# Pooled attention and two MLPs on one core: the order of weight conversion, u3 and the first evacuation in the second MLP

## The chip, the cores and the metric

One core of one Trainium2 chip runs the whole program. The metric is device time in microseconds (us) of one execution; lower is better. Engines are called as in the profile: PE is TensorE (matmul), DVE is VectorE, ACT is ScalarE, POOL is GpSimd, SP is the queue that issues the loads.

## What is computed

```python
q_pool = q.reshape(B, H, S // 2, 2, D).mean(axis=3)
attn = softmax(scale * q_pool @ k^T);  x = (attn @ v)          # 1152 tokens x 512
h = x @ w_in;  r = np.maximum(h, 0.0);  g = s * (r * r) + b    # 512 -> 2048
x = g @ w_out                                                  # 2048 -> 512
a = x @ w_a;  b = x @ w_b;  out = (a * b) @ w_out2             # 512 -> 1536 -> 512
```

[...]

## The kernel before

Every product is made from two parts of each operand: a rounded part h and the rest l, as h*h + h*l + l*h, three matmuls into one PSUM sum (`mm3`, L616). A **unit** is one megabyte of float64 weights. `units` (L104) lists 34 of them: 16 of the first MLP (index 0 to 15), 12 of the second (16 to 27, alternating w_a and w_b), 6 of the last matrix. Converting unit i has two phases, which the generator `conv_phases` (L177) hands out one after the other:

- **bits** (L187): ACT scales the upper words into the tile f (L143), DVE shifts (L145) and joins the lower words (L147), SP's next load is issued (`unit_load`, L128), and for the second MLP DVE makes four sums of blocks (`conv_sums`, L149).
- **split** (L196): ACT rounds f into wh and the sums into sh (L168), DVE or POOL makes wl and sl (L173).

The first MLP walks over `order1`, one unit per step i, two column blocks (mm 0 and 1) per step; in the last steps DVE adds the PSUM results into xacc (L741). `mlp1` yields "split" at the start of a step and "bits" behind the first column block, and the loop at L853 answers each with one conversion phase (two at step 14). So split and bits of coming units stand in the engines' queues between the evacuations: program order is each engine's order here (`manual_schedule`). Behind the evacuations x2's parts are made for the second MLP (`x_sums`, L782): casts x2h on ACT (L772), differences on DVE (L776, L769).

The second MLP multiplies 2 by 2 blocks by seven products instead of eight (p1 to p7, table `FORM`, L833), 12 matmuls of 288 columns each, accumulated in four PSUM pairs of banks. Its unit n (0 to 11) is index 16 + n of the list, odd n are w_b. From n = 1 on the loop at L969 writes PE's order p1, p6, p2, p7, p5, p4, p3. Between the products stand the evacuations: u1 copied by ACT (L848), u2 and **u3** added by DVE (`add_up`, L851), and four results `to(n, i, z)`. p4 accumulates on the bank pair that u3 is read from, so p4 waits for u3. For odd n each result is multiplied by the one of the unit before, by POOL (`times`, L922); the first result, `evac11` (L916), is an exception: for odd n DVE multiplies it straight from PSUM, for even n ACT copies it.

During unit n the conversion of unit n + 1 runs: DVE's L145 and L147 at its start, the sums behind u2, ACT's wh and sh behind these, DVE's wl in two halves of 512 columns, sl (x2l for odd units) on POOL. p6 of unit n + 1 reads sl. The tile f of these units lies in PSUM.

Of the kernel before, what the change touches and what calls it, by code (L numbers as in the profile page):

```python
# [9 lines left out]
F32 = mybir.dt.float32  # L10
F32R = mybir.dt.float32r
I32 = mybir.dt.int32
I64 = mybir.dt.int64
AF = mybir.ActivationFunctionType
ALU = mybir.AluOpType
# [27 lines left out]
def kernel(  # L43
# [14 lines left out]
    nc = tc.nc  # L58
# [4 lines left out]
    SP = S // 2  # L63
# [7 lines left out]
    HC = SP // 2  # L71
# [9 lines left out]
    sp_ps = [ctx.enter_context(tc.tile_pool(name="sp0", bufs=1))]  # L81
    cv_ps = [ctx.enter_context(tc.tile_pool(name="cv0", bufs=1))]
# [21 lines left out]
    units = []  # L104
# [6 lines left out]
    for up, c, u in order1:  # L111
        if up:
            w = w_in[:, c * 512 + u * 256:c * 512 + (u + 1) * 256]
        else:
            w = w_out[c * 512:(c + 1) * 512, u * 256:(u + 1) * 256]
        units.append([(slice(0, 1024), w.rearrange("(k p) f -> p k f", p=128))])
    N1 = len(units)
# [6 lines left out]
    raw_t = {}  # L124
# [3 lines left out]
    def unit_load():  # L128
        i = st["load"]
        z = (i + 1) % 2 if i else 0  # L130
        if i >= len(units) or z >= len(raw_ps):
            return
        t = raw_ps[z].tile([128, 1024], I64, tag="raw", name="raw")
        for c, src in units[i]:
            nc.sync.dma_start(out=t[:, c].rearrange("p (k f) -> p k f", f=src.shape[-1]), in_=src)
        raw_t[i] = t
        st["load"] += 1

    def conv_bits(f, raw):
        words = raw.bitcast(I32).rearrange("p (n t) -> p n t", t=2)  # L140
        lo, hi = words[:, :, 0], words[:, :, 1]

        nc.scalar.activation(out=f.bitcast(F32), in_=hi.bitcast(F32), func=AF.Prelu, scale=2.0 ** -112, alpha=2.0 ** 32)  # L143
        yield
        nc.vector.tensor_scalar(out=f, in0=f, scalar1=3, scalar2=None, op0=ALU.logical_shift_left)  # L145
        yield
        nc.vector.scalar_tensor_tensor(out=f, in0=lo, scalar=29, in1=f, op0=ALU.logical_shift_right, op1=ALU.bitwise_or)  # L147

    def conv_sums(f, t):  # L149

        f = f.bitcast(F32).rearrange("p (k f) -> p k f", k=4)
        a11, a12, a21, a22 = (f[:, 2 * y:2 * y + 2, 128 * x:128 * x + 128] for x in range(2) for y in range(2))
        if f.space == PSUM:
            a = ss_ps[0].tile([128, 2, 128], F32, tag="a21", name="a21")
            nc.scalar.copy(out=a, in_=a21)
        else:
            a = a21
        yield
        for out, x, y, op in (
            (t[:, 1], a11, a, ALU.subtract), (a21, a22, a, ALU.add),  # L160
            (t[:, 0], a22, t[:, 1], ALU.subtract), (t[:, 2], a12, t[:, 0], ALU.subtract),
        ):
            nc.vector.tensor_tensor(out=out, in0=x, in1=y, op=op)  # L163
            yield

    def round_h(h, f, eng):
        if eng is nc.scalar:
            nc.scalar.copy(out=h, in_=f)  # L168
        else:
            nc.gpsimd.tensor_scalar(out=h, in0=f, scalar1=1.0, scalar2=0.0, op0=ALU.mult, op1=ALU.add)  # L170

    def round_l(l, f, h, eng):
        eng.tensor_tensor(out=l, in0=f, in1=h.bitcast(F32), op=ALU.subtract)  # L173

    w2_at = {}

    def conv_phases():  # L177

        for i in range(len(units)):
            in_psum = N1 + 2 <= i <= N2  # L180
            if in_psum:
                f = ps2[3].tile([128, 2, 512], F32, tag="pp", name="f").rearrange("p a n -> p (a n)").bitcast(I32)
            else:
                f = cv_ps[i % len(cv_ps)].tile([128, 1024], I32, tag="f", name="f")
            t = ss_ps[i % 2].tile([128, 3, 2, 128], F32, tag="t", name="t") if N1 <= i < N2 else None

            def bits():  # L187
                yield from conv_bits(f, raw_t.pop(i))
                unit_load()
                yield  # L190
                if i < N1:
                    yield
                if t is not None:
                    yield from conv_sums(f, t)

            def split_up():  # L196
                eng = nc.gpsimd if i < N1 - 1 else nc.scalar
                if i < N2 + 2:
                    p = sp_ps[i % 2]
                    parts = tuple(p.tile([128, 1024], F32R, tag=f"w{x}", name=f"w{x}") for x in "hl")  # L200
                else:
                    parts = w2_room[i - N2 - 2]
                x = f.bitcast(F32)
                round_h(parts[0], x, eng)
                yield
                more = ()
                if t is not None:
                    if i % 2:
                        more = tuple(x[:, 0:768].rearrange("p (z k f) -> p z k f", z=3, k=2) for x in x_room["odd"])
                    else:  # L210
                        more = tuple(ss_ps[0].tile([128, 3, 2, 128], F32R, tag=f"s{x}", name=f"s{x}") for x in "hl")
                    round_h(more[0], t, eng)
                    yield
                if i < N2:
                    sp_t.append(parts + more)
                else:
                    for k in range(2):
                        w2_at[2 * (i - N2) + k] = [x[:, 512 * k:512 * k + 512] for x in parts]
                if in_psum:
                    for c in (slice(0, 512), slice(512, 1024)):  # L220
                        round_l(parts[1][:, c], x[:, c], parts[0][:, c], nc.vector)
                        yield
                else:
                    round_l(parts[1], x, parts[0], nc.vector if t is not None else nc.gpsimd)
                    yield
                if t is not None:
                    round_l(more[1], t, more[0], nc.gpsimd if in_psum else nc.vector)
                    yield

            yield bits()  # L230
            yield split_up()

    ss_ps, w2_room, x_room, ps2 = [], [], {}, []
    phases = conv_phases()
# [2 lines left out]
    def conv_step(n=1, steps=conv):  # L237
        for _ in range(n):
            next(steps, None)
# [386 lines left out]
    with tc.manual_schedule():  # L626
# [193 lines left out]
        def halves(t):  # L820
            return t.rearrange("p (a n) -> p a n", a=2)
# [14 lines left out]
        def product(ps, w, name, first=True):  # L836
            a, x = FORM[name]
            for k in range(2):
                mm3([ps[:, i, 0:HC] for i in range(2)], [t[:, k] for t in w[a]], x_at(x, k), first and k == 0, k == 1, first is not True)
# [72 lines left out]
        def to(n, i, z):  # L912
            p, mul = divmod(n, 2)
            return halves((ab_at(2 * p + i) if mul else at[i])[:, z * SP:(z + 1) * SP])

        def evac11(n, ps):  # L916
            if n % 2:
                nc.vector.tensor_tensor(out=to(n, 0, 0), in0=ps[:, :, 0:HC], in1=halves(at[0][:, 0:SP]), op=ALU.mult)
            else:
                nc.scalar.copy(out=to(n, 0, 0), in_=ps[:, :, 0:HC])  # L920

        def times(n, i, z):  # L922
            if n % 2:
                nc.gpsimd.tensor_tensor(
                    out=to(n, i, z), in0=to(n, i, z), in1=halves(at[i][:, z * SP:(z + 1) * SP]), op=ALU.mult
                )
# [42 lines left out]
        for n in range(1, NU):  # L969

            w = unit_blocks()
            last = n == NU - 1
            a = pair(2)
            product(a, w, "p1")
            if n > 1:
                conv_step(2, ahead)
            copy_up("u1", a)
            b = pair(1)
            product(b, w, "p6")
            if n > 1:  # L980
                conv_step(1, ahead)
            add_up(u_tile("u2"), b, U["u1"])
            conv_step(9, ahead)
            ahead = next(phases)
            conv_step(3 if last else 2, ahead)
            product(a, w, "p2", False)
            if last:
                ab_split(0)
            else:
                conv_step(1, ahead)  # L990
            product(b, w, "p7", False)
            add_up(u_tile("u3"), b, U["u1"])
            conv_step(9, ahead)
            c = pair(0)
            product(c, w, "p5")
            add_up(to(n, 1, 1), c, U["u3"])
            times(n, 1, 1)
            evac11(n, a)
            if last:
                ab_split(1)  # L1000
            product(b, w, "p4", False)
            add_up(to(n, 1, 0), b, U["u1"])
            times(n, 1, 0)
            product(c, w, "p3", False)
            ahead = next(phases)
            conv_step(1, ahead)
            add_up(to(n, 0, 1), c, U["u2"])
            times(n, 0, 1)
# [63 lines left out]
```

## Time and profile before

| what | value |
|---|---|
| median of 3 runs | 711.39 us (709.99 to 711.54) |
| profiled execution, its own time | 711.81 us |
| span of that execution | 710.0 us |
| PE busy | 681.6 us, 96% of the span |
| DVE, ACT, POOL busy | 528.6 us (74%), 396.2 us (56%), 371.9 us (52%) |
| mean granted clock of PE | 0.992 |

The profile is one execution; its rows give start and length in us from the start of the span. A bracket behind a row tells how long the engine was idle before it and which instruction ended that. Consecutive equal instructions are merged in a row, with their count.

### The profile page before, as it was taken

The numbers are of one execution on the slowest core, as the hardware profiler recorded it, in microseconds if no ns is written. First come the engines' busy times: TensorE is split into PE (matmuls) and PEld (weight loads), VectorE is DVE, ScalarE is ACT, GpSimd is POOL, SyncE is SP. The second block draws the span as 40 slices with busy tenths as digits, with TensorE's granted clock in tenths as the row PEclk, the third lists the DMA queues.
The fourth block names the chain that finished last, engine by engine and source line by source line (L and its number), as shares of the span: only waits on it lengthen the run. The fifth ranks groups of instructions, "written<-read, shape, count | busy, mean of one in ns | idle before, by whom it ended". The sixth has DMA issues, their size and how long they took to land.

```text
span 710.0 us, 11849 instructions
## 1 busy us (share of the span) xinstructions
PE 681.6 (96%) x4446; PEld 651.0 (92%) x4446; DVE 528.6 (74%) x963; ACT 396.2 (56%) x861; POOL 371.9 (52%) x372
## 2 busy tenths in 40 slices
PE   7999999999999999999999999988899999999994
PEld 6899999999999989999999999978899999988883
DVE  5999999999999995774375465589778787887430
ACT  5998999999999984553343224135243333444220
POOL 4879797988879775683545455100332433142200
PEclk9999999999999999999999999999999999999998
DMA  6122120302121004322323131310232222322012
GB/s 225 35 67 66 38 69 31 102 12 91 35 67 35 1 24 140 107 88 72 106 63 117 60 119 59 119 60 0 74 105 81 98 91 89 98 96 104 0 47 86
DMA packets 26013, 52.93 MB, mean 75 GB/s; under 512 B 1636, under 2 KB 2916, under 8 KB 25956
## 3 DMA queue, kind: packets, MB, share of 16 engines
q1 hardware_dynamic: 25826, 52.04, 22.4%
q8 instruction: 35, 0.57, 0.3%
q14 instruction: 22, 0.18, 0.1%
q10 hardware_dynamic: 130, 0.13, 0.1%
HBM read 49.81 MB, written 2.36 MB: 73 GB/s over the span
## 4 chain that ended last, share of the span: by engine, by line
PE 71%; DVE 18%; ACT 6%; issue 2%; POOL 1%; DMA 0%; DVEq 0%; ACTq 0%
PE ps L623 26%; PE pp L907 10%; PE pp L623 9%; PE pv L508 9%; PE t L474 7%; PE s L399 6%; PE s L406 3%; DVE p3l L492 2%; DVE t L163 2%; DVE u L851 2%; ACT wh L168 2%; DVE sm L425 2%; PE t L344 1%; DVE wl L173 1%; DVE f L145 1%
## 5 line engine op out<-in xcount | busy, mean ns | idle before, releaser
L474 PE MATMUL t<-ident,e 128*128 128x128 f32 x648 | 98.6, 275 | 3.1 <-DVE p2l L492 1.3
L457 POOL TENSOR_SCALAR e<-e,sm 128x1152 f32<-128x1152 f32 x72 | 88.7, 1233 | 11.5 <-DVE sm L452 6.7
L474 PEld LDWEIGHTS t<-ident,e 128*128 128x128 f32 x648 | 75.2, 140 | 13.5 <-DVE sm L430 2.2
L732 POOL TENSOR_SCALAR r<-r,sb_s,sb_b 128x384 f32<-128x384 f32 (+1 forms) x46 | 41.1, 906 | 55.2 <-DVE r L729 55.2
L422 DVE TENSOR_REDUCE sm<-s 128x1 f32<-128x768 f32 x72 | 68.2, 948 | 1.8 <-PE s L399 1.8
L492 DVE TENSOR_TENSOR p3l<-t,p3h 128x512 fp32r<-128x512 f32 (+1 forms) x120 | 64.2, 553 | 7.0 <-ACT p3h L486 4.5
L441 ACT ACTIVATE e<-s,sm 128x768 f32<-128x768 f32 x72 | 66.5, 924 | 0.0
L486 ACT CAST p3h<-t 128x512 fp32r<-128x512 f32 (+1 forms) x120 | 56.2, 485 | 5.5 <-PE t L474 3.2
L173 POOL TENSOR_TENSOR sl<-t,sh 128x768 fp32r<-128x768 f32 x5 | 9.2, 1843 | 90.8 <-ACT sh L168 90.8
L726 ACT ACTIVATE r<-ps 128x384 f32<-128x384 f32 (+1 forms) x46 | 20.1, 505 | 61.7 <-PE ps L623 61.6
L623 PE MATMUL pp<-x2h,wh 128*128 128x288 f32 x192 | 43.5, 308 | 10.5 <-DVE u L851 5.4
L729 DVE SCALAR_TENSOR_TENSOR r<-ps,r 128x384 f32<-128x384 f32 (+1 forms) x46 | 23.8, 567 | 37.1 <-ACT r L726 37.1
L492 DVE TENSOR_TENSOR p2l<-t,p2h 128x512 fp32r<-128x512 f32 x96 | 50.6, 548 | 1.0 <-ACT p2h L486 0.8
L173 POOL TENSOR_TENSOR wl<-f,wh 128x1024 fp32r<-128x1024 f32 x17 | 42.9, 2525 | 9.4 <-ACT wh L168 8.2
L486 ACT CAST p2h<-t 128x512 fp32r<-128x512 f32 x96 | 44.8, 501 | 5.1 <-PE t L474 4.5
L508 PE MATMUL pv<-p3h,v 128*128 128x320 f32 x144 | 47.6, 338 | 0.0
L434 ACT ACTIVATE e<-s,sm 128x384 f32<-128x384 f32 x72 | 43.0, 597 | 7.5 <-DVE sm L452 3.5
L143 ACT ACTIVATE f<-raw 128x1024 f32<-128x1024 f32 x34 | 38.7, 1139 | 14.4 <-issue 6.7
L145 DVE TENSOR_SCALAR f<-f 128x1024 int32<-128x1024 int32 x34 | 37.9, 1116 | 11.6 <-ACT f L143 11.5
L147 DVE SCALAR_TENSOR_TENSOR f<-raw,f 128x1024 int32<-128x1024 int32 x34 | 45.6, 1342 | 1.1
L623 PE MATMUL ps<-xa_h,wh 128*128 128x384 f32 (+1 forms) x200 | 45.3, 330 | 0.1
L623 PE MATMUL ps<-xa_h,wl 128*128 128x384 f32 (+1 forms) x200 | 45.0, 328 | 0.0
(144 smaller groups left out, 2095.5 us busy)
## 6 DMA issues: line engine op xcount, KB each, us to landing
raw<-in_moe_w_out_dram SPq DMA_DIRECT2D x14, 1024.0 KB, 4.9
raw<-in_moe_w_in_dram SPq DMA_DIRECT2D x8, 1024.0 KB, 5.6
raw<-in_moe_w_a_dram SPq DMA_DIRECT2D x6, 1024.0 KB, 5.0
raw<-in_moe_w_b_dram SPq DMA_DIRECT2D x6, 1024.0 KB, 5.6
vn<-in_v_dram SPq DMA_DIRECT2D x8, 576.0 KB, 3.9
kn<-in_k_dram SPq DMA_DIRECT2D x7, 576.0 KB, 3.9
qn<-in_q_dram SPq DMA_DIRECT2D x7, 512.0 KB, 3.7
out_dram<-ab SPq DMA_DIRECT2D x8, 256.0 KB, 2.7
```

The lines of the kernel that those rows point to most:

```text
L145: nc.vector.tensor_scalar(out=f, in0=f, scalar1=3, scalar2=None, op0=ALU.logical_shift_left)
L147: nc.vector.scalar_tensor_tensor(out=f, in0=lo, scalar=29, in1=f, op0=ALU.logical_shift_right, op1=ALU.bitwise_or)
L173: eng.tensor_tensor(out=l, in0=f, in1=h.bitcast(F32), op=ALU.subtract)
L422: nc.vector.reduce_max(small(g)[:, 0:1], SPS[g, 0][:, :, 0:384], axis=AX.XY)
L441: nc.scalar.activation(out=e_tile(g)[:, 0:768].rearrange("p (a c) -> p a c", a=2), in_=SPS.pop((g, 0))[:, :, 0:384], func=AF.Exp, bias=m[: ...
L457: nc.gpsimd.tensor_scalar(out=e, in0=e, scalar1=m[:, 6:7], scalar2=1.0, op0=ALU.mult, op1=ALU.mult)
L474: nc.tensor.transpose(ps[:, i * 128:(i + 1) * 128], E[g][:, (c0 + i) * 128:(c0 + i + 1) * 128], ident)
L486: nc.scalar.copy(out=p_dst(g)[0][:, c0:c0 + n], in_=p_src(g, z))
L492: nc.vector.tensor_tensor(out=l, in0=p_src(g, z), in1=h.bitcast(F32), op=ALU.subtract)
L508: nc.tensor.matmul(ps[:, 0:N], V[n, hd][:, c].rearrange("p a d -> p (a d)"), p, start=(t == 0), stop=(t == 2 * NC - 1))
L623: nc.tensor.matmul(ps, a, c[:, o:o + n], start=(first and z == 0), stop=(last and z == 2), skip_group_check=more)
L907: nc.tensor.matmul(ps, a[x], w2_at[kf][c], start=(kf == 0 and y == 0), stop=(kf == KF2 - 1 and y == 2))
```

## The change

Three things. First, the order in which `conv_phases` hands out the phases: for index 16 the split is kept back until the bits of index 17 are done. Second, in the loop over n `add_up(u_tile("u3"), ...)` now stands ahead of both halves of wl, and the second half (with sl on POOL) behind `to(n, 1, 1)` and its multiplication. Third, `evac11` is an ACT copy for every n and is put right behind p2; for odd n POOL multiplies the copied result (`times(n, 0, 0)`). `round_h` is written out in place, the `yield` behind the copy of a21 now stands for PSUM units alone.

```diff
+    def conv_phases():
+        late = []
         for i in range(len(units)):
...
+            bits, split_up = conv_unit(i)
+            yield bits
+            yield from late
+
+            late = [split_up] if i == N1 else []
+            if not late:
+                yield split_up
...
         def evac11(n, ps):
-            if n % 2:
-                nc.vector.tensor_tensor(out=to(n, 0, 0), in0=ps[:, :, 0:HC], in1=halves(at[0][:, 0:SP]), op=ALU.mult)
-            else:
-                nc.scalar.copy(out=to(n, 0, 0), in_=ps[:, :, 0:HC])
+            nc.scalar.copy(out=to(n, 0, 0), in_=ps[:, :, 0:HC])
+            times(n, 0, 0)
...
-            conv_step(3 if last else 2, ahead)
+            conv_step(1 if last else 2, ahead)
             product(a, w, "p2", False)
+            evac11(n, a)
             if last:
                 ab_split(0)
-            else:
-                conv_step(1, ahead)
             product(b, w, "p7", False)
             add_up(u_tile("u3"), b, U["u1"])
-            conv_step(9, ahead)
+            conv_step(1, ahead)
             c = pair(0)
             product(c, w, "p5")
             add_up(to(n, 1, 1), c, U["u3"])
             times(n, 1, 1)
-            evac11(n, a)
+            conv_step(9, ahead)
```

**DVE at the seam of the two MLPs** (steps 14 and 15 of the first MLP; wl and sl are the split of index 16, L145 to L163 the bits of index 17, xacc<-ps the evacuations). Before:

```order
L741 TENSOR_TENSOR xacc<-ps_5868,xacc 128x384
L173 TENSOR_TENSOR wl<-f,wh 128x1024
L173 TENSOR_TENSOR sl<-t,sh 128x768
L776 TENSOR_TENSOR x2l<-xacc,x2h 128x576
L769 TENSOR_TENSOR xacc<-xacc 128x576
...
L145 TENSOR_SCALAR f<-f 128x1024
L147 SCALAR_TENSOR_TENSOR f<-raw,f 128x1024
L163 TENSOR_TENSOR t<-f 128x256
L163 TENSOR_TENSOR f<-f 128x2x128
L163 TENSOR_TENSOR t<-f,t 128x256 x2
L741 TENSOR_TENSOR xacc<-ps_5979,xacc 128x384
```

Now, the same stretch of DVE:

```order
L746 TENSOR_TENSOR xacc<-ps_5868,xacc 128x384
L145 TENSOR_SCALAR f<-f 128x1024
L147 SCALAR_TENSOR_TENSOR f<-raw,f 128x1024
L163 TENSOR_TENSOR t<-f 128x256
L163 TENSOR_TENSOR f<-f 128x2x128
L163 TENSOR_TENSOR t<-f,t 128x256 x2
L781 TENSOR_TENSOR x2l<-xacc,x2h 128x576
...
L167 TENSOR_TENSOR wl<-f,wh 128x1024
L167 TENSOR_TENSOR sl<-t,sh 128x768
L746 TENSOR_TENSOR xacc<-ps_5979,xacc 128x384
```

The bits of 17 and the split of 16 have changed places; what lies between them is as it was. On ACT the scaling of 17 (L143) moves in front of four casts x2h, and wh and sh of 16 behind these.

**DVE in unit 3 of the second MLP** (u_6533 before and u_6535 now are u3, `ab<-pp,u` the results). Before:

```order
L163 TENSOR_TENSOR t<-f,t 128x256 x2
L173 TENSOR_TENSOR wl<-f,wh 128x512
L851 TENSOR_TENSOR u_6533<-pp,u_6479 128x576
L173 TENSOR_TENSOR wl<-f,wh 128x512
L851 TENSOR_TENSOR ab<-pp,u_6533 128x576
L918 TENSOR_TENSOR ab<-pp,at 128x576
L851 TENSOR_TENSOR ab<-pp,u_6479 128x576
```

Now:

```order
L163 TENSOR_TENSOR t<-f,t 128x256 x2
L856 TENSOR_TENSOR u_6535<-pp,u_6480 128x576
L167 TENSOR_TENSOR wl<-f,wh 128x512
L856 TENSOR_TENSOR ab<-pp,u_6535 128x576
L167 TENSOR_TENSOR wl<-f,wh 128x512
L856 TENSOR_TENSOR ab<-pp,u_6480 128x576
```

u3 stands in front of the half of wl that it stood behind, and the multiplication from PSUM (L918) is gone from DVE.

**POOL from unit 1 to unit 2 of the second MLP** (ab<-ab,at are the multiplications of an odd unit, sl belongs to the even unit that follows, x2l to the odd one). Before:

```order
L173 TENSOR_TENSOR sl<-t,sh 128x768
L924 TENSOR_TENSOR ab<-ab,at 128x576 x3
L173 TENSOR_TENSOR x2l<-t,x2h 128x768
```

Now:

```order
L927 TENSOR_TENSOR ab<-ab,at 128x576 x2
L167 TENSOR_TENSOR sl<-t,sh 128x768
L927 TENSOR_TENSOR ab<-ab,at 128x576 x2
L167 TENSOR_TENSOR x2l<-t,x2h 128x768
```

In an odd unit POOL now has four multiplications instead of three, and sl waits behind two of them. PE's and SP's orders are unchanged.

## Rows read from the trace of the kernel before

**Rows 1.** Waits of PE, whole span: us in total, times, longest.
```profile
PE pp L623 <- DVE u L851: 5.4, 10, 2.8
```
**Rows 2.** Timeline of PE, second MLP: start, length, engine, line, [idle before <-releaser].
```profile
477.45 0.82 PE L623 MATMUL pp<-x2h,wh 128*128 128x288 f32 x2 [2.60 <-DVE xacc L741]
...
483.91 0.53 PE L623 MATMUL pp<-x2h,wh 128*128 128x288 f32 x2 [1.58 <-ACT u L848]
...
504.08 0.54 PE L623 MATMUL pp<-x2h,wh 128*128 128x288 f32 x2 [2.83 <-DVE u L851]
...
508.90 0.43 PE L623 MATMUL pp<-x2h,wh 128*128 128x288 f32 x2
...
517.34 0.53 PE L623 MATMUL pp<-x2h,wh 128*128 128x288 f32 x2 [0.29 <-DVE u L851]
...
611.06 0.54 PE L623 MATMUL pp<-x2h,wh 128*128 128x288 f32 x2 [0.30 <-DVE u L851]
...
614.36 0.43 PE L623 MATMUL pp<-x2h,wh 128*128 128x288 f32 x2
...
625.52 0.39 PE L907 MATMUL pp<-wh,x2h 128*128 128x512 f32 x1
```
**Rows 3.** Windows: PE, PEld, DVE, ACT, POOL busy (count), granted clock, DMA share, GB/s.
```profile
477.50:480.50 3.00, 3.00 (x13) 3.00 (x14) 2.92 (x5) 1.41 (x4) 0.00 (x0) 0.50 0.40 156
480.50:504.00 23.50, 18.31 (x133) 17.60 (x132) 21.12 (x32) 11.51 (x17) 0.55 (x1) 1.00 0.13 45
504.50:507.90 3.40, 3.40 (x16) 3.40 (x16) 2.21 (x4) 1.14 (x1) 2.29 (x3) 0.51 0.00 0
```
**Rows 4.** Timelines of ACT (first row) and of DVE at the seam.
```profile
461.09 1.05 ACT L168 CAST wh<-f 128x1024 fp32r<-128x1024 f32 x1 [10.42 <-PE ps L623]
...
455.56 1.48 DVE L741 TENSOR_TENSOR xacc<-ps,xacc 128x384 f32<-128x384 f32 x3
462.17 1.23 DVE L173 TENSOR_TENSOR wl<-f,wh 128x1024 fp32r<-128x1024 f32 x1 [5.13 <-ACT wh L168]
...
475.82 1.48 DVE L741 TENSOR_TENSOR xacc<-ps,xacc 128x384 f32<-128x384 f32 x3
```
**Rows 5.** Waits from 455 to 477 us: PE's weight loads.
```profile
PEld ps L623 <- DVE xacc L741: 0.8, 3, 0.3
```
**Rows 6.** Timeline of DVE, unit 1: last sums and u3.
```profile
500.71 0.88 DVE L163 TENSOR_TENSOR t<-f,t 128x256 f32<-128x256 f32 x2
...
503.28 0.75 DVE L851 TENSOR_TENSOR u<-pp,u 128x576 f32<-128x576 f32 x1
```
**Rows 7.** Timeline of ACT: casts in unit 1, copy in unit 2.
```profile
501.63 1.01 ACT L168 CAST wh<-f 128x1024 fp32r<-128x1024 f32 x1 [1.88 <-DVE t L163]
502.54 0.83 ACT L168 CAST sh<-t 128x768 fp32r<-128x768 f32 x1
...
516.53 0.64 ACT L920 COPY at<-pp 128x576 f32<-128x576 f32 x1
```
**Rows 8.** Timeline of POOL, unit 3.
```profile
528.41 1.85 POOL L173 TENSOR_TENSOR sl<-t,sh 128x768 fp32r<-128x768 f32 x1 [9.86 <-ACT sh L168]
530.33 2.88 POOL L924 TENSOR_TENSOR ab<-ab,at 128x576 f32<-128x576 f32 x2
```
**Rows 9.** Timelines of ACT (first row) and of DVE, unit 11: splits of two results.
```profile
618.73 2.21 ACT L94 CAST x2h<-ab 128x1152 fp32r<-128x1152 f32 x2
...
620.07 1.35 DVE L99 TENSOR_TENSOR x2l<-ab,x2h 128x1152 fp32r<-128x1152 f32 x1
...
623.86 2.15 DVE L99 TENSOR_TENSOR x2l<-ab,x2h 128x1152 fp32r<-128x1152 f32 x1
```
**Rows 10.** Timeline of POOL and of PE at the end of the second MLP.
```profile
623.36 1.44 POOL L924 TENSOR_TENSOR ab<-ab,at 128x576 f32<-128x576 f32 x1 [11.09 <-DVE ab L851]
...
626.76 3.27 POOL L924 TENSOR_TENSOR ab<-ab,at 128x576 f32<-128x576 f32 x2 [1.96 <-DVE ab L851]
...
637.87 0.51 PE L907 MATMUL pp<-wh,x2l 128*128 128x512 f32 x1 [0.82 <-DVE x2l L99]
```

More of the change, by code (lines that the diff above doesn't have):

```diff
@@ L155, in conv_sums @@
             nc.scalar.copy(out=a, in_=a21)
+            yield
         else:
             a = a21
-        yield
         for out, x, y, op in (
@@ L164, in conv_sums @@
             yield
-    def round_h(h, f, eng):
-        if eng is nc.scalar:
-            nc.scalar.copy(out=h, in_=f)
-        else:
-            nc.gpsimd.tensor_scalar(out=h, in0=f, scalar1=1.0, scalar2=0.0, op0=ALU.mult, op1=ALU.add)
     def round_l(l, f, h, eng):
@@ L175, with conv_unit, bits, split_up @@
     w2_at = {}
+    def conv_unit(i):
+        in_psum = N1 + 2 <= i <= N2
+        if in_psum:
+            f = ps2[3].tile([128, 2, 512], F32, tag="pp", name="f").rearrange("p a n -> p (a n)").bitcast(I32)
+        else:
+            f = cv_ps[i % len(cv_ps)].tile([128, 1024], I32, tag="f", name="f")
+        x = f.bitcast(F32)
+        t = ss_ps[i % 2].tile([128, 3, 2, 128], F32, tag="t", name="t") if N1 <= i < N2 else None
+        def bits():
+            yield from conv_bits(f, raw_t.pop(i))
+            unit_load()
+            yield
+            if i < N1:
+                yield
+            if t is not None:
+                yield from conv_sums(f, t)
+        def split_up():
+            if i < N2 + 2:
+                p = sp_ps[i % 2]
+                parts = [p.tile([128, 1024], F32R, tag=f"w{z}", name=f"w{z}") for z in "hl"]
+            else:
+                parts = w2_room[i - N2 - 2]
+            if i < N1 - 1:
+                nc.gpsimd.tensor_scalar(out=parts[0], in0=x, scalar1=1.0, scalar2=0.0, op0=ALU.mult, op1=ALU.add)
+            else:
+                nc.scalar.copy(out=parts[0], in_=x)
+            yield
+            more = []
+            if t is not None:
+                if i % 2:
+                    more = [z[:, 0:768].rearrange("p (z k f) -> p z k f", z=3, k=2) for z in x_room["odd"]]
+                else:
+                    more = [ss_ps[0].tile([128, 3, 2, 128], F32R, tag=f"s{z}", name=f"s{z}") for z in "hl"]
+                nc.scalar.copy(out=more[0], in_=t)
+                yield
+            if i < N2:
+                sp_t.append(parts + more)
+            else:
+                for k in range(2):
+                    w2_at[2 * (i - N2) + k] = [z[:, 512 * k:512 * k + 512] for z in parts]
+            if in_psum:
+                for c in (slice(0, 512), slice(512, 1024)):
+                    round_l(parts[1][:, c], x[:, c], parts[0][:, c], nc.vector)
+                    yield
+            else:
+                round_l(parts[1], x, parts[0], nc.vector if t is not None else nc.gpsimd)
+                yield
+            if t is not None:
+                round_l(more[1], t, more[0], nc.gpsimd if in_psum else nc.vector)
+                yield
+        return bits(), split_up()
@@ L177, in conv_phases @@
     def conv_phases():
+        late = []
         for i in range(len(units)):
-            in_psum = N1 + 2 <= i <= N2
-            if in_psum:
-                f = ps2[3].tile([128, 2, 512], F32, tag="pp", name="f").rearrange("p a n -> p (a n)").bitcast(I32)
-            else:
[L184 to L228, printed above, removed]
@@ L230, in conv_phases @@
-            yield bits()
-            yield split_up()
+            bits, split_up = conv_unit(i)
[4 more added lines that the diff above has]
+                yield split_up
     ss_ps, w2_room, x_room, ps2 = [], [], {}, []
@@ L916, in evac11 @@
         def evac11(n, ps):
-            if n % 2:
-                nc.vector.tensor_tensor(out=to(n, 0, 0), in0=ps[:, :, 0:HC], in1=halves(at[0][:, 0:SP]), op=ALU.mult)
-            else:
-                nc.scalar.copy(out=to(n, 0, 0), in_=ps[:, :, 0:HC])
+            nc.scalar.copy(out=to(n, 0, 0), in_=ps[:, :, 0:HC])
+            times(n, 0, 0)
         def times(n, i, z):
@@ L984 @@
             ahead = next(phases)
-            conv_step(3 if last else 2, ahead)
+            conv_step(1 if last else 2, ahead)
             product(a, w, "p2", False)
+            evac11(n, a)
             if last:
                 ab_split(0)
-            else:
-                conv_step(1, ahead)
             product(b, w, "p7", False)
             add_up(u_tile("u3"), b, U["u1"])
-            conv_step(9, ahead)
+            conv_step(1, ahead)
             c = pair(0)
```

## The prediction

> **What bounds the kernel now.** I read PE's waits first: PE is busy 96% of the span, so only time in which it stands still, or runs at half clock, can be won. That time has three causes where the change works. (a) In the second MLP PE waits ten times for an addition u by DVE [rows 1]; its timeline [rows 2] shows one wait of 2.83 in unit 1 and waits of 0.29 or 0.30 from unit 2 (517.34) to unit 10 (611.06), all at p4, which needs u3 to have read its banks. (b) At the seam PE waits 2.60 for an evacuation by DVE (477.45) and 1.58 for a copy by ACT (483.91) [rows 2]. (c) Behind the two longest of these gaps the granted clock is 0.50 and 0.51, that is 1.2 instead of 2.4 GHz; over the stretch that holds the 1.58 it is 1.00 [rows 3].
>
> Then DVE's timeline at the seam [rows 4]. DVE is done with an evacuation at 457.04 (455.56 + 1.48) and stands still for 5.13, until ACT has cast wh of index 16; that cast starts at 461.09, behind PE, whose last products read the same buffer. From there DVE is dense, and everything to p4 of unit 1 hangs on it: the evacuation that releases p1 comes only at 475.82. Even PE's weight loads in the last product of the first MLP wait 0.8 for a late evacuation [rows 5].
>
> **The change, part by part.**
>
> *Seam.* The bits of 17 need nothing of PE. They need their raw load, which SP issues behind the bits of 15, and their tile f, which POOL frees with wl of 15; in the timelines of SP and POOL both are over well before 457. So DVE can fill its 5.13. From 462.17 to 475.82 it ran split, x2's differences, one evacuation and the bits, 13.65 in all [rows 4]. The same instructions now start at 457.04 and take 13.65: the evacuation of 475.82 starts at 470.7, 5.1 earlier. Bounds: 3.4, if only PE's own waits go (2.60 and the 0.8 of [rows 5]) and p2 of unit 0 keeps its place behind ACT; 5.4, if the short wait of DVE between split and bits goes too. I take **5.1**, since ACT and DVE behind 475.82 keep their order and p2's 1.58 is a wait for that chain, not for PE. The half clock at 477.5 to 480.5 goes with its gap, but wins nothing of its own: PE comes to p2 sooner and waits there as before.
>
> *u3 ahead of wl.* In unit 1 the last sum ends at 501.59 (500.71 + 0.88) and u3 starts at 503.28, behind wh on ACT and a half of wl [rows 6]. p7 is done by then, so u3 moves up by **1.69**. PE's wait falls to 1.1, less than the 1.58 that left the clock alone. At full clock p4 and p3 take two sevenths of a unit: unit 11, which has no wait, takes 11.16 (614.36 to 625.52), so 3.2 and 0.1 for the restart, against 4.82 (504.08 to 508.90) [rows 2]: **1.5** more, 0 if the clock falls all the same.
>
> In units 2 to 10 a unit takes 11.715 ((611.06 - 517.34) / 8), against 11.16 without a wait [rows 2]. u3's end lies 2.44 behind the last sum now (1.69 + 0.75 [rows 6]) and p4 starts 8.44 behind p1 (508.90 to 517.34), so the last sum ends some 6.0 behind p1. u3 then starts when p7 is done (6.4 + 0.25 until DVE has it) and ends at 7.4; p4 is due at 8.0. The whole 0.55 goes, 9 times: **5.0**. The halves of wl now stand behind u3 and behind the next result; the first reader of the second half is p2 of the next unit, over 4 us later, and p3, which waits for the result between them (ends near 9.0), is due at 9.6.
>
> *First result by ACT, multiplied by POOL.* DVE loses a multiplication in odd units, ACT gains a copy of 0.64 [rows 7], behind its casts, where it then only waits for a PSUM tile: nothing on the path. POOL gains 1.44 per odd unit [rows 8], and this has a price: sl now stands behind the copy and two multiplications. From the last sum to sl's end: wh to sh 0.91, sh 0.83, copy 0.64 [rows 7], two multiplications 2.88, sl 1.85 [rows 8], handovers 0.15: 7.25, where it was 3.7. In steady state that is 6.0 + 7.25 = 13.25 behind p1; p6 of the next unit wants sl in its third of six rows, at 11.16 + 1.6 + 0.53 = 13.3. It just holds. In unit 1 it doesn't: the last sum ends at 501.59 - 5.1 = 496.5, sl at 503.7; p1 of unit 2 starts at 508.90 - 5.1 - 1.7 - 1.5 = 500.6, p6's third row is due at 502.7. **+1.0** there. This wait also takes up the 1.5 of the clock: if the clock falls in unit 1 after all, this wait goes instead. For units 3, 5, 7, 9: 0, up to 0.35 each if the multiplications take 1.64, as beside DVE at the end (3.27 for two) [rows 10].
>
> *Last unit.* The copy now stands ahead of ACT's casts of the first two results, and x2l ahead of u3. p2 of unit 11 is done at 619.4; copy 0.64, cast 1.1 [rows 9]: x2l starts at 621.1. It takes 1.35, or 2.15 when POOL multiplies beside it [rows 9, 10], then u3 0.75: p4 starts at 623.2 to 624.0 instead of 622.3. u3, the halves of wl and the next result then push the second x2l from 623.86 to about 625.3, and with it the chain that ends in PE's wait of 0.82 at 637.87 [rows 10]. Bounds 1.0 (x2l alone) and 1.9 (both x2l slowed); I take **+1.4**, between them, since POOL's multiplication, behind the same copy, overlaps the first x2l in part. The Trainium skill ("SBUF — State Buffer", "SBUF: two separate sides") says that a DVE instruction with two SBUF inputs and a POOL instruction that reads SBUF exclude each other for the whole instruction. The trace agrees: the x2l of 2.15 ended at 626.01, 1.21 behind the end of POOL's multiplication of 623.36. By this rule the new multiplication (620.1 to 621.5) holds x2l up by 0.4, and the sum has 1.4 here; if the two shared the time freely, it would have 1.0.
>
> **Sum.** -5.1 - 1.7 - 1.5 + 1.0 - 5.0 + 1.4 = -10.9. The profiled execution took 711.81, so 700.9; the median of the runs, 711.39, lies 0.4 below it, and what is measured is a median: **700.5**. Its own range is 699.5 to 702.0 (about 1.4 us, 0.2%, is what a measurement of this kernel can tell from no change).
>
> **Rivals.**
>
> *POOL sets the pace* (0.14). For: sl has under 0.1 of slack in odd units. Against: POOL's durations hardly vary in these units. With 1.64 per multiplication: 0.35 in four units and 0.4 in unit 1, 1.8: 702.3.
>
> *The clock falls behind the shorter gaps* (0.12). At the seam four gaps of about 1 us now follow each other within 25 us (p2 of units 0 and 1, p4 of 1, p6 of 2). Against: at 480.5 to 504.0 two such gaps left it at 1.00 [rows 3]. A spell like that of unit 1 costs 1.5 where no later wait takes it up: 702.0, two 703.5. The Trainium skill ("TensorE: Matmul & The Clock Gate", "A second HAM failure mode: psum-queue depth-cycling") tells of short idle times between groups of matmuls that make the clock swing; by that rule this case comes true; no row here shows it for gaps of this length.
>
> *The seam gives only PE's own waits* (0.08), 3.4 instead of 5.1: 702.2.
>
> *The last unit costs nothing* (0.06), its wait swallowed by the one at 637.87: 699.1.
>
> *Slower* (0.03). The clock stays at half through whole units of the second MLP. A unit is 84 matmuls; the 12 of p4 and p3 lost 1.5 in unit 1, so a whole unit loses some 10. From 1.1 units on the gain of 10.9 is gone; two units give 720. Against it: the units themselves lose their gaps.
>
> *It doesn't do what it says* (0.03): the bits of 17 wait for their load or for f, DVE stands still as before, and the odd units give back to POOL what they win: 710 to 711.5.
>
> **Chances and range.** The forecast itself 0.54. Faster by over 0.2%: all but the last two, 0.94; within 0.2% 0.03; slower 0.03. The range, 699.0 to 703.6, leaves out the last two, two spells of half clock with something beside, and the forecast's own tails.
>
> **What would show it.** DVE without the idle 5.13 and L145 of 17 at 457; p1 of unit 0 without a wait, p2 of unit 0 about 5 earlier; u3 right behind the last sum in unit 1 and no wait at p4 in units 2 to 10, p1 to p1 in 11.2; one wait of about 1 at p6 of unit 2 for sl; a new wait at p4 of unit 11; granted clock 1.00 from the seam on. Wrong would be: a wait for sl at p6 of every even unit, a half clock behind 1 us gaps, or p2 of unit 0 less than 4 earlier.

## The result, and the profile after

The changed kernel takes 700.12 us (median of 4 runs, 699.38 to 700.60), the kernel before 711.18 us beside it (4 runs, 709.99 to 711.54). The ratio is 0.9846, 95% interval 0.9829 to 0.9863: faster by 11.1 us, where 10.9 was forecast, and inside the range.

The profiled execution took 700.22 us, its span is 698.4 us (before 711.81 and 710.0). The first two lines are the page's busy times of the change, the rest its waits of PE in the second MLP (us in total, times, longest). Lines of the file are five higher than before: L628 is L623, L856 is L851, L167 is L173.

```profile
span 698.4 us, 11847 instructions
...
PE 676.6 (97%) x4446; PEld 648.7 (93%) x4446; DVE 524.4 (75%) x957; ACT 399.6 (57%) x867; POOL 379.4 (54%) x378
```

```profile
PE pp L628 <- ACT u L853: 2.2, 2, 1.3
PE pp L628 <- DVE u L856: 2.0, 2, 1.0
...
PE pp L912 <- DVE x2l L99: 1.0, 1, 1.0
...
PE pp L628 <- POOL sl L167: 0.6, 1, 0.6
```

Of the ten waits for u3 [rows 1] one is left, at p4 of unit 1, and the wait for an evacuation at the seam is gone. Two waits are new: 0.9 for u3 at p4 of unit 11, and 0.6 for sl. The timeline of PE in the changed kernel shows where they stand (start, length, engine, line, [idle before <-releaser]):

```profile
478.18 0.53 PE L628 MATMUL pp<-x2h,wh 128*128 128x288 f32 x2 [1.34 <-ACT u L853]
...
490.45 0.53 PE L628 MATMUL pp<-x2h,wh 128*128 128x288 f32 x2 [0.83 <-ACT u L853]
...
496.56 0.53 PE L628 MATMUL pp<-x2h,wh 128*128 128x288 f32 x2 [1.05 <-DVE u L856]
...
500.02 0.42 PE L628 MATMUL pp<-x2h,wh 128*128 128x288 f32 x2
...
502.90 0.54 PE L628 MATMUL pp<-x2h,sl 128*128 128x288 f32 x2 [0.60 <-POOL sl L167]
...
512.04 0.43 PE L628 MATMUL pp<-x2h,wh 128*128 128x288 f32 x2
...
601.43 0.43 PE L628 MATMUL pp<-x2h,wh 128*128 128x288 f32 x2
...
610.52 0.53 PE L628 MATMUL pp<-x2h,wh 128*128 128x288 f32 x2 [0.94 <-DVE u L856]
...
626.31 0.50 PE L912 MATMUL pp<-wh,x2l 128*128 128x512 f32 x1 [0.96 <-DVE x2l L99]
```

In order of time these are p2 of unit 0, p2 of unit 1, p4 of unit 1, p1 of unit 2, p6 of unit 2 (its matmul with sl), p1 of units 3 and 11, p4 of unit 11, and the wait in the output product for the third x2l, which DVE makes behind the second one and the bits of two further units. Between units 3 and 11 PE waits no more. The timeline of DVE at the seam, against [rows 4]:

```profile
455.15 1.48 DVE L746 TENSOR_TENSOR xacc<-ps,xacc 128x384 f32<-128x384 f32 x3
456.54 0.68 DVE L145 TENSOR_SCALAR f<-f 128x1024 int32<-128x1024 int32 x1
...
468.08 1.23 DVE L167 TENSOR_TENSOR wl<-f,wh 128x1024 fp32r<-128x1024 f32 x1 [0.19 <-ACT wh L199]
...
470.09 1.48 DVE L746 TENSOR_TENSOR xacc<-ps,xacc 128x384 f32<-128x384 f32 x3
```

The shift L145 of index 17 runs straight behind the evacuation, where DVE stood still for 5.13 us, and wl follows with 0.19 of idle time. From one evacuation to the other it is 14.94 (470.09 - 455.15), where it was 20.26 (475.82 - 455.56). The granted clock in two windows of the changed kernel (columns as in [rows 3]):

```profile
477.40:500.20 22.80, 20.14 (x146) 19.53 (x147) 20.47 (x29) 11.46 (x17) 1.96 (x2) 1.00 0.15 47
497.00:505.00 8.00, 7.40 (x55) 7.03 (x54) 6.32 (x8) 3.29 (x5) 6.76 (x5) 1.00 0.19 60
```

It is 1.00, that is 2.4 GHz, over all four shorter gaps. Term by term, the two profiled executions against each other (one execution each, so a few tenths are chance):

| term | predicted | measured | from |
|---|---|---|---|
| seam | -5.1 | -5.3 | evacuation to evacuation 20.26 to 14.94 |
| u3 in unit 1 | -1.7 | -1.8 | p2 of unit 0 to p4 of unit 1: 20.17 to 18.38 |
| clock in unit 1 | -1.5 | -1.4 | p4 of unit 1 to p1 of unit 2: 4.82 to 3.46 |
| sl in unit 2 | +1.0 | +0.8 | p1 of unit 2 to p1 of unit 3: 12.02, where the units behind it take 11.17 |
| units 2 to 10 | -5.0 | -4.9 | 11.715 to 11.17 ((601.43 - 512.04) / 8), nine times |
| last unit | +1.4 | +1.4 | p1 of unit 11 to the end of the output's wait: 23.51 to 24.88 |

That makes -11.2. The other 0.4 of the 11.6 between these two executions lies ahead of the change: the evacuation that the seam starts from begins 0.41 earlier.

### The profile page after: what moved, and what is told of

Read it like the earlier page. It is cut to its first block, busy times and chain, and to the rows that moved or that the text cites. A ratio compares the mean times of both kernels' runs of the same rounds, so it can differ in the third digit from the quotient of the medians.

```text
span 698.4 us, 11847 instructions
## 1 busy us (share of the span) xinstructions
PE 676.6 (97%) x4446; PEld 648.7 (93%) x4446; DVE 524.4 (75%) x957; ACT 399.6 (57%) x867; POOL 379.4 (54%) x378
## 4 chain that ended last, share of the span: by engine, by line
PE 79%; DVE 12%; ACT 4%; POOL 2%; issue 1%; DMA 0%; SPq 0%; ACTq 0%; POOLq 0%
PE ps L628 24%; PE pp L628 15%; PE pp L912 11%; PE pv L513 9%; PE t L479 8%; PE s L404 7%; PE s L411 3%; DVE p3l L497 2%; DVE sm L430 1%; PE t L349 1%; PE t L369 1%; DVE x2l L781 1%; DVE xs L532 1%; ACT p3h L491 1%; POOL e L462 1%
## 5 line engine op out<-in xcount | busy, mean ns | idle before, releaser
L927 POOL TENSOR_TENSOR ab<-ab,at 128x576 f32<-128x576 f32 x24 | 34.4, 1452 | 98.4 <-ACT ab L922 93.2
L143 ACT ACTIVATE f<-raw 128x1024 f32<-128x1024 f32 x34 | 38.7, 1140 | 18.9 <-issue 12.8
L167 POOL TENSOR_TENSOR wl<-f,wh 128x1024 fp32r<-128x1024 f32 x17 | 42.9, 2523 | 9.4 <-ACT wh L199 8.2
L145 DVE TENSOR_SCALAR f<-f 128x1024 int32<-128x1024 int32 x34 | 37.8, 1112 | 11.4 <-ACT f L143 11.2
L628 PE MATMUL pp<-x2h,wh 128*128 128x288 f32 x192 | 41.5, 297 | 4.2 <-ACT u L853 2.2
L628 PE MATMUL ps<-xa_h,wh 128*128 128x384 f32 (+1 forms) x200 | 45.3, 330 | 0.1
L628 PE MATMUL ps<-xa_h,wl 128*128 128x384 f32 (+1 forms) x200 | 45.0, 328 | 0.0
```

The source lines that it names most:

```text
L628: nc.tensor.matmul(ps, a, c[:, o:o + n], start=(first and z == 0), stop=(last and z == 2), skip_group_check=more)
```

## The experiments

What the total does not tell is whether each part is worth what its term says, and whether the third part, the copy by ACT with its multiplication on POOL, pays for the wait for sl and the last unit. The theory is the sum as predicted; the rivals are those of the prediction. The kernel before took 711.47 us (17 runs, 710.01 to 712.97) beside the first four kernels below, and 711.65 us (9 runs, 710.38 to 713.01) beside the other four.

**The seam alone** (`e1_seam`): the kernel before with this part of the diff only.

```diff
+        late = []
         for i in range(len(units)):
...
+            bits, split_up = conv_unit(i)
+            yield bits
+            yield from late
+
+            late = [split_up] if i == N1 else []
+            if not late:
+                yield split_up
```

> The seam alone: bits of 17 ahead of the split of 16, u3 and evac11 as before. The theory of separate terms: DVE loses its idle 5.1, p2 of unit 0 comes 5.1 to 5.4 earlier, the wait of 2.83 at p4 of unit 1, the half clock behind it and the nine waits of 0.29 stay: 711.2 - 5.3 = 705.9. Rival, the seam's gain ends up in the next wait: p4 of unit 1 waits longer and the time is 709 to 711. Rival, only PE's own waits go: 707.8.

Measured: 705.62 us (6 runs, 703.85 to 707.25), ratio 0.9918 (0.9901 to 0.9935). DVE's evacuations stand 14.96 apart (454.41 and 469.37), as in the change: the whole 5.3 belongs to the order of bits and split. Its timeline of PE at p4 of unit 1, and the window behind that wait:

```profile
497.63 0.54 PE L628 MATMUL pp<-x2h,wh 128*128 128x288 f32 x2 [2.81 <-DVE u L856]
```

```profile
497.50:500.90 3.40, 3.27 (x24) 3.27 (x25) 2.76 (x5) 1.11 (x1) 3.31 (x3) 1.00 0.00 0
```

The gap is as long as in the kernel before, and behind it the clock is 1.00, where it was 0.51 [rows 3]. From p2 of unit 0 to the end of the span this execution takes 224.5 (before 226.1): 1.5 less with the same waits. So the length of the gap alone doesn't bring the half clock: it came behind this gap in one profiled execution and not in the other. The six runs of this kernel go with their mean granted clock in the main, from 703.85 us at 0.997 to 707.25 us at 0.988.

**u3 alone** (`e2_u3`): the kernel before with u3 ahead of both halves of wl; the first result and the last unit as before.

```diff
-            else:
-                conv_step(1, ahead)
             product(b, w, "p7", False)
             add_up(u_tile("u3"), b, U["u1"])
-            conv_step(9, ahead)
+            if not last:
+                conv_step(1, ahead)
...
             times(n, 1, 1)
+            conv_step(9, ahead)
             evac11(n, a)
```

> u3 ahead of both halves of wl alone, the first result of odd units still multiplied by DVE from PSUM, the seam and the last unit as before. Separate terms: the 2.83 at p4 of unit 1 falls by 1.7 and with it the half clock (1.4), the nine short waits go (4.8 to 5.0), sl stands behind one multiplication and is not waited for: 711.2 - 8.0 = 703.2, with the 2.60 at p1 of unit 0 and its half clock still there. Rival, u3 wins only if DVE also loses the multiplication: the waits at p4 stay in odd units, 707 to 711. Rival, the clock falls behind the gap of 1.1 as well: 704.6.

Measured: 702.54 us (4 runs, 702.30 to 703.76), ratio 0.9877 (0.9863 to 0.9891). At p4 of unit 1 PE waits 1.06 for u3, at p4 of units 2 to 10 not at all, though DVE still multiplies the first result from PSUM in odd units: that multiplication was on no path. The granted clock at the seam, with the same 2.6 gap as before, and from there on:

```profile
477.50:480.50 3.00, 3.00 (x13) 3.00 (x14) 2.93 (x5) 1.41 (x4) 0.00 (x0) 0.50 0.41 159
480.50:504.00 23.50, 19.99 (x145) 19.20 (x144) 21.80 (x33) 11.50 (x17) 0.00 (x0) 1.00 0.14 45
```

It is half behind the long gap and 1.00 in the stretch that holds the 1.06.

**The first result alone** (`e3_evac`): the kernel before with ACT copying the first result behind p2 and POOL multiplying it in every odd unit.

```diff
         def evac11(n, ps):
-            if n % 2:
-                nc.vector.tensor_tensor(out=to(n, 0, 0), in0=ps[:, :, 0:HC], in1=halves(at[0][:, 0:SP]), op=ALU.mult)
-            else:
-                nc.scalar.copy(out=to(n, 0, 0), in_=ps[:, :, 0:HC])
+            nc.scalar.copy(out=to(n, 0, 0), in_=ps[:, :, 0:HC])
+            times(n, 0, 0)
...
             product(a, w, "p2", False)
+            evac11(n, a)
...
-            evac11(n, a)
```

> evac11 alone: ACT copies the first result of every unit behind p2, POOL multiplies it in odd units, u3 and the seam as before. Separate terms: the nine waits at p4 stay as they are (u3 still behind wl), sl stands behind one multiplication and keeps its slack, and the last unit loses 1.2 to 1.4 because the copy stands ahead of ACT's casts and x2l ahead of u3: 711.2 + 1.3 = 712.5. Rival, DVE's 0.75 per odd unit was on the path: 6 x 0.75 less, 706.7 to 708.

Measured: 711.07 us (12 runs, 710.24 to 712.95), ratio 0.9996 (0.9986 to 1.0007): no difference, where 712.5 was expected. The new wait at p4 of unit 11 is there, but the wait of 0.82 before the output [rows 10] is gone. PE and DVE in unit 11:

```profile
613.05 0.43 PE L623 MATMUL pp<-x2h,wh 128*128 128x288 f32 x2
...
622.13 0.54 PE L623 MATMUL pp<-x2h,wh 128*128 128x288 f32 x2 [0.95 <-DVE u L851]
```

```profile
619.76 1.65 DVE L99 TENSOR_TENSOR x2l<-ab,x2h 128x1152 fp32r<-128x1152 f32 x1 [0.91 <-ACT x2h L94]
...
622.85 1.35 DVE L99 TENSOR_TENSOR x2l<-ab,x2h 128x1152 fp32r<-128x1152 f32 x1
```

Counted from p1 of unit 11 (613.05 here, 614.36 before [rows 2]), the second x2l starts 0.3 later than before, but takes 1.35, not 2.15 [rows 9], and so ends 0.5 earlier. Here both halves of wl still run ahead of u3; in the change they stand behind it and push the second x2l. So the loss in the last unit needs two parts of the change together, which the expectation had missed. Behind a gap of 2.83 at p4 of unit 1 the clock is 1.00 in this execution too (last line below). Behind the 2.61 at the seam it fell, but not at once, as the first two lines show:

```profile
477.50:480.50 3.00, 2.88 (x17) 2.91 (x18) 2.75 (x5) 1.42 (x3) 0.00 (x0) 0.75 0.48 186
480.50:504.00 23.50, 18.54 (x129) 17.72 (x128) 21.13 (x32) 12.13 (x19) 0.00 (x0) 0.96 0.14 44
504.50:507.90 3.40, 3.40 (x27) 3.40 (x27) 1.87 (x4) 1.13 (x1) 3.40 (x3) 1.00 0.00 0
```

**Seam and u3, without the first result** (`e4_seam_u3`): the two edits of `e1_seam` and `e2_u3` in one kernel.

> The seam and u3 together, evac11 and the last unit as before the change. Separate terms: the changed kernel less its two new waits, 0.7 at p6 of unit 2 for sl and 1.4 in the last unit: 700.1 - 2.1 = 698.0, with no wait for sl (one multiplication ahead of it) and none at p4 of unit 11. Rival, the three edits need each other (DVE's multiplication comes back on the path in odd units): 700.1 or more, with waits at p4 or p3 of odd units.

Measured: 697.48 us (5 runs, 697.25 to 698.56), ratio 0.9808 (0.9794 to 0.9821). It is faster than the change, whose runs all lie above it. Its waits of PE in the second MLP, and POOL in unit 1:

```profile
PE pp L628 <- ACT u L853: 2.2, 2, 1.4
PE pp L628 <- DVE u L856: 1.1, 1, 1.1
PE pp L912 <- DVE x2l L99: 0.8, 1, 0.8
```

```profile
497.72 1.43 POOL L929 TENSOR_TENSOR ab<-ab,at 128x576 f32<-128x576 f32 x1 [46.69 <-DVE ab L856]
499.11 1.84 POOL L167 TENSOR_TENSOR sl<-t,sh 128x768 fp32r<-128x768 f32 x1
```

With one multiplication ahead of it sl ends at 500.95, and PE has no wait for it. So the third part of the change costs 2.6 us on top of the first two (700.12 - 697.48; 2.9 by the gain of each over the kernel before beside it). From p2 of unit 0 to the end of the span it is 2.1 (220.2 in the change, 218.1 here): 0.8 by the wait for sl and 1.4 in the last unit. The rest is no more than runs differ: the profiled executions are 0.7 apart at p2 of unit 0 already, up to which the two kernels are the same.

**The last unit** (`e5_last`): the change, with the copy of unit 11's first result behind ACT's cast of the first x2h instead of behind p2.

```diff
             product(a, w, "p2", False)
-            evac11(n, a)
             if last:
                 ab_split(0)
+            else:
+                evac11(n, a)
...
             times(n, 1, 1)
+            if last:
+                evac11(n, a)
             conv_step(9, ahead)
```

> The changed kernel, but in the last unit the copy of the first result stands behind ACT's cast for the first x2l, where the multiplication stood before; all else as changed. My theory: x2l of the first result starts about 1.5 earlier, p4 of unit 11 loses its wait of 0.94, and from p1 of unit 11 to the end of PE's wait in the output product it takes 23.5 as before the change instead of 24.9: 700.1 - 1.4 = 698.7. Rival, the wait at p4 only moves into the next wait (x2l of the third result): that grows and the time stays at 699.6 to 700.1.

Measured: 698.42 us (4 runs, 697.46 to 699.05), ratio 0.9811 (0.9796 to 0.9825). The waits of 0.94 and 0.96 are both gone and that for sl stays. PE at p6 of unit 2, and DVE's first x2l:

```profile
502.99 0.53 PE L628 MATMUL pp<-x2h,sl 128*128 128x288 f32 x2 [0.61 <-POOL sl L167]
```

```profile
607.08 1.36 DVE L99 TENSOR_TENSOR x2l<-ab,x2h 128x1152 fp32r<-128x1152 f32 x1 [1.34 <-ACT x2h L94]
```

DVE waits 1.34 for the cast x2h here and 2.51 in the change: the copy ahead of ACT's casts is what made u3 late.

**More work for POOL** (`e6_pool`): how much slack has sl in the other units?

```diff
             times(n, 1, 1)
+            if n % 2 and not last:
+                times(n, 1, 1)
             conv_step(9, ahead)
```

> The changed kernel with one multiplication more on POOL ahead of sl in units 1, 3, 5, 7, 9: the result (1,1) is multiplied by its partner twice, so that block is computed otherwise. If sl has only some 0.15 of slack, as the changed kernel's rows show (sl ends at 525.00, its weights are loaded at about 525.16), each of p6 of units 4, 6, 8, 10 waits 1.28 and p6 of unit 2 another 1.41: 700.1 + 6.5 = 706.6. Rival, POOL has room (slack over 1): 700.1 to 702.

Measured: 708.43 us (5 runs, 705.98 to 708.96), ratio 0.9954 (0.9941 to 0.9968). Its waits of PE for sl, one of them in the timeline, and POOL ahead of it:

```profile
PE pp L628 <- POOL sl L167: 6.3, 5, 2.1
```

```profile
527.08 0.53 PE L628 MATMUL pp<-x2h,sl 128*128 128x288 f32 x2 [1.04 <-POOL sl L167]
```

```profile
520.90 4.34 POOL L927 TENSOR_TENSOR ab<-ab,at 128x576 f32<-128x576 f32 x3 [9.85 <-ACT ab L922]
```

A multiplication of 1.44 makes PE wait 1.04 in unit 4, where it waited for nothing: sl's slack in the change is some 0.4 (1.44 - 1.04). The profiled execution took 705.98, 5.8 more than that of the change, about the waits' growth of 5.7. The other four runs took over 2 us more, three of them at a mean granted clock of 0.990 where the profiled one had 0.995; where in them the time went no row shows.

**The first result by ACT and POOL in the last unit alone** (`e7_best`): `e4_seam_u3`, with unit 11's first result copied behind the cast and multiplied by POOL.

```diff
-            if n % 2:
+            if n == KF2 - 1:
+                nc.scalar.copy(out=to(n, 0, 0), in_=ps[:, :, 0:HC])
+                times(n, 0, 0)
+            elif n % 2:
```

> The seam and u3 with evac11 as before, but for the last unit, where ACT copies the first result behind its cast for the first x2l and POOL multiplies it. DVE has the second x2l 0.75 earlier and so the chain to PE's wait of 0.82 in the output product, as in the run with evac11 alone, where this wait was gone while p4 of unit 11 waited 0.95: here neither wait, 697.5 - 0.8 = 696.7. Rival, POOL's multiplication slows the second x2l as it did and the wait stays: 697.5.

Measured: 697.42 us (4 runs, 696.73 to 697.51), ratio 0.9796 (0.9782 to 0.9809). By time it can't be told from `e4_seam_u3`. Its profile has neither wait of the last unit. DVE has lost the multiplication ahead of the second x2l, and this x2l now starts ahead of POOL's first multiplication (610.00) and takes 1.35; in `e4_seam_u3` it starts behind it and takes 2.15:

```profile
609.84 1.35 DVE L99 TENSOR_TENSOR x2l<-ab,x2h 128x1152 fp32r<-128x1152 f32 x1
```

From p2 of unit 0 to the end of the span it takes 217.1 against 218.1, 1.0 less where 0.8 was expected; in this execution its start up to the seam took 1.06 longer, in stretches where the two kernels are the same.

**sl ahead of the first result's multiplication** (`e8_sl`): the change, with this multiplication behind sl in POOL's order.

```diff
             nc.scalar.copy(out=to(n, 0, 0), in_=ps[:, :, 0:HC])
-            times(n, 0, 0)
...
             conv_step(9, ahead)
+            times(n, 0, 0)
```

> The changed kernel, but POOL multiplies the first result of odd units behind sl instead of ahead of it. My theory: sl comes 1.4 earlier, the wait of 0.60 at p6 of unit 2 (0.74 with its restart) goes and no other unit changes: 700.1 - 0.7 = 699.4, the last unit still with its loss of 1.4. Rival, the wait goes into p7 or p4 of unit 2, where the sums come no earlier: 700.1.

Measured: 697.67 us (4 runs, 697.48 to 697.77), ratio 0.9801 (0.9787 to 0.9814), 1.7 better than expected. The wait for sl is gone, and the last unit got better without being meant. DVE there:

```profile
606.53 1.36 DVE L99 TENSOR_TENSOR x2l<-ab,x2h 128x1152 fp32r<-128x1152 f32 x1 [2.50 <-ACT x2h L94]
...
613.80 0.68 DVE L145 TENSOR_SCALAR f<-f 128x1024 int32<-128x1024 int32 x1
```

POOL there, its second and third multiplication in one row:

```profile
611.28 4.49 POOL L926 TENSOR_TENSOR ab<-ab,at 128x576 f32<-128x576 f32 x2
```

The same two instructions of DVE in the change, and POOL's multiplications beside them:

```profile
608.16 1.64 DVE L99 TENSOR_TENSOR x2l<-ab,x2h 128x1152 fp32r<-128x1152 f32 x1 [2.51 <-ACT x2h L94]
...
615.70 1.48 DVE L145 TENSOR_SCALAR f<-f 128x1024 int32<-128x1024 int32 x1
```

```profile
607.14 1.44 POOL L927 TENSOR_TENSOR ab<-ab,at 128x576 f32<-128x576 f32 x1 [7.24 <-ACT ab L922]
...
615.19 3.27 POOL L927 TENSOR_TENSOR ab<-ab,at 128x576 f32<-128x576 f32 x2 [1.96 <-DVE ab L856]
```

In the change POOL multiplies until 608.58, into the first x2l, which takes 1.64; in `e8_sl` POOL has nothing to do then, and x2l takes 1.36. Further on the two engines have changed parts. In the change POOL is at work from 615.19 when the shift L145 comes at 615.70 and takes 1.48; in `e8_sl` L145 comes as POOL's second multiplication ends (613.84) and the third begins (613.79), and takes 0.68. POOL needs 4.49 for these two, where two take 2.82 in unit 1 of the change: 2.56 for the second, beside the second x2l, and 1.98 for the third, beside L145. By x2l (0.28) and L145 (0.80) p4 of unit 11 waits 0.66 (0.94 in the change) and the output 0.22 (0.96), 1.0 less together. The profiled execution is also 0.8 ahead at p2 of unit 0 already (477.40, in the change 478.18), up to which the two kernels are the same; that is about the rest.

Three kernels, `e4_seam_u3`, `e7_best` and `e8_sl`, are thus faster than the change by 2.5 to 2.7 us, and their medians lie within 0.25 of each other. They were not run beside the change; against the kernel before beside them they gain 14.0 to 14.2, the change 11.1. What PE still waits for in all of them is 1.3 at p2 of unit 0, 0.8 at p2 of unit 1 and 1.1 at p4 of unit 1, behind DVE's and ACT's chain from the seam. To shorten that chain was not tried.

## Why the prediction was right

**The seam** came out as predicted, 5.3 for 5.1, near the upper bound of 5.4: DVE's 5.13 is filled, and its short wait between split and bits fell from 0.29 to 0.19. DVE was not dense there, though the prediction says so: some 2.1 of the 13.65 were waits for ACT, which moved along nearly whole (1.95 in the change). PE's own waits would have given 3.4; that rival falls. `e1_seam` shows the same 5.3 with nothing else changed.

**u3**: 1.8 for 1.7 in unit 1, 4.9 for 5.0 in units 2 to 10. `e2_u3` shows that the place of the halves of wl alone is enough. The two parts together (`e4_seam_u3`) take 14.0 off the median of before; one by one they take 5.9 and 8.9.

**The clock** was the weakest term. Between the two profiled executions it is there, 1.4 for 1.5. But the prediction took it as what a gap of 2.83 costs, and `e1_seam` and `e3_evac` have gaps of 2.81 and 2.83 with a granted clock of 1.00 behind them. It is what such a gap costs in some executions. The medians speak for more than the waits: `e2_u3` is 8.9 below the kernel before (7.8 to 9.7 by its interval), and the waits that it takes away come to 6.7 (1.8 and 4.9). That the rest is the clock is not shown. It is in part luck that one execution of each kernel gave 1.4 for 1.5.

**The wait for sl** came where it was put, p6 of unit 2, at 0.8 for 1.0, since sl ended at 502.85 (501.02 + 1.83 in POOL's timeline, below) instead of 503.7, while p1 of unit 2 came 0.6 earlier than the 500.6 worked out for it.

```profile
498.24 2.82 POOL L927 TENSOR_TENSOR ab<-ab,at 128x576 f32<-128x576 f32 x2 [46.53 <-ACT ab L922]
501.02 1.83 POOL L167 TENSOR_TENSOR sl<-t,sh 128x768 fp32r<-128x768 f32 x1
```

In the other units sl was said to hold with under 0.1; `e6_pool` makes it 0.4. The rival *POOL sets the pace* was refuted for this change, and its mechanism shown at once: one multiplication more, and POOL does set it. The rival *Slower* counts 12 matmuls in p4 and p3; they are 24, so by its own reckoning a unit at half clock loses some 5, not 10. The forecast does not rest on it.

**The last unit** cost 1.4, as predicted, by the path predicted: x2l ahead of u3, then the halves of wl ahead of the second x2l. The first x2l took 1.64, 0.29 longer than beside an idle POOL; POOL's multiplication of 607.14 ended at 608.58, 0.42 behind the start of x2l at 608.16. The Trainium skill ("SBUF — State Buffer", "SBUF: two separate sides") lets, of a DVE instruction with two SBUF inputs and a POOL instruction that reads SBUF, the one that starts first have the port for its whole instruction, which would give the whole 0.42; the trace has most of it.

**The clock behind the shorter gaps** did not fall: 1.00 over gaps of 0.60 to 1.34, so that rival falls, and with it the swing that the Trainium skill ("TensorE: Matmul & The Clock Gate", "A second HAM failure mode: psum-queue depth-cycling") describes is not seen here. Nor did the units run at half clock, and the bits of 17 waited for no load.

What the prediction did not say, though its own terms held it: the third part had a price, 1.0 and 1.4, and nothing on the other side. It was argued to take nothing off the path, and `e4_seam_u3` shows just that.

## What to carry to other kernels

Where an engine waits in its order of the program, later work that waits for nothing belongs into the gap; and an operation on whose reading another engine waits goes ahead of those whose results are wanted much later. Work moved to an engine that has time to spare is not free: look at what stands behind it in that engine's order, by when that is wanted, and at the last pass of the loop, where the order differs; if the engine that it leaves was not on the path, the move can only cost. A term that rests on the clock behind a gap in one profiled execution wants a second execution.

## What the runs showed of the hardware

The granted clock after a gap of PE is not the same each time. Behind the gap at the seam (2.60, 2.58 and 2.61 us) it fell in all three profiled executions that have it, at once in two of them (0.50) and later in `e3_evac` (0.75 over the first 3 us). Behind the longer gap at p4 of unit 1 it was 0.51 in one execution (2.83) and 1.00 in two (2.81 and 2.83). So the length of the gap alone does not decide. The runs of `e1_seam`, with the gap of 2.81, lie between 703.85 and 707.25 (6 runs); those of the change and of the four kernels without a gap over 1.4 (`e4_seam_u3`, `e5_last`, `e7_best`, `e8_sl`) lie within 0.3 to 1.6 of each other (4 or 5 runs each). `e2_u3`, with the gap of 2.58, has 1.5, so a long gap need not make them differ; the executions without a profile have no rows to show where their clock fell.

DVE and POOL slow each other, and for the x2l the one that comes second is held. The x2l takes 1.35 us alone, 1.64 with 0.42 of POOL's multiplication ahead of it, and 2.15 in unit 11 of the kernel before, where the multiplication has 0.94 to go [rows 9, 10]. In `e7_best` it comes 0.16 ahead of a multiplication and takes 1.35, and the multiplication takes 2.47 instead of 1.43. The shift L145 takes 1.48 when POOL is at work already, and 0.68 where one multiplication ends and the next begins; the next then takes 1.98. In `e8_sl` this was worth 1.0 of the wait at p4 of unit 11 and at the output (0.28 and 0.74), more than the wait of 0.6 for sl that was to be removed.
